# A state-space scan in front of a squared-ReLU layer: the first loads reordered, unit 0's masks on one engine, and the order of work up to unit 5 written anew

## The chip, the cores and the metric

One Trainium2 chip, one of its cores. The metric is the time of one execution on the device in microseconds (us). The engines of the core run side by side, each through its own list of instructions in order: TensorE (PE in the profile; PEld is its weight load), VectorE (DVE), ScalarE (ACT), GpSimd (POOL) and SyncE (SP). SP, ACT and POOL issue DMA transfers; SPq, ACTq and POOLq are the rows of these issues. An instruction waits at the head of its engine's list until what it reads is there and what it overwrites has been read; everything behind it on that engine waits too.

## The reference

Inputs: x (4 batches, 8 heads, 768 steps, 32 wide), a (4, 8, 768), B and C (4, 8, 768, 16), w_in (256 x 2048), w_out (2048 x 256), all fp32. Per batch and head, over the steps in chunks of 32:

```python
log_a = np.log(np.clip(a, 1e-06, 1.0))
cum = np.cumsum(la, axis=-1)                       # la: log_a of this chunk
L = np.exp(cum[:, :, :, None] - cum[:, :, None, :]) * causal
M = np.einsum('bhin,bhjn->bhij', Cc, Bc) * L
y_intra = np.einsum('bhij,bhjd->bhid', M, xc)
y_inter = np.einsum('bhin,bhnd->bhid', Cc, state) * np.exp(cum)[:, :, :, None]
y[:, :, sl] = y_intra + y_inter
state = decay_full * state + np.sum(Bx, axis=2)    # Bx: outer(B, x), decayed to the chunk's end
```

Then y is laid out as 3072 tokens of 256 numbers, and the result is `relu(y @ w_in)**2 @ w_out`, 3072 x 256 in fp32.

## The kernel before, in words

**Units.** The 768 steps are cut into three parts of 256 (j), and a unit is one part of one batch: 12 units, numbered 0 to 11 as (b, j) with the batch running fastest, so units 0 to 3 are the first 256 steps of the four batches. A part of 256 steps is two chunks of 128 in the kernel's sense (i = 0, 1), and a state goes from chunk to chunk. Even and odd steps lie side by side in one partition (the index r, 0 or 1).

**Decay.** The products of a are taken as a running product rather than as sums of logarithms. `a_nat[0]` (64 partitions x 128) holds a of units 0 to 3, `a_nat[1]` (128 x 128, "late a") that of all others. `clamp` (L473) limits it, `scan` (L479) runs the product along 128 steps into `cp`; both are on VectorE. `prep_p` (L455) transposes `cp` on TensorE; for units 0 to 3 the result P0 is in PSUM bank 4 (token `sp`), for the rest it is `P_sb[:, :, 32:96]` (token `p`). `inv` (L560) takes reciprocals into `Pinv`. Totals of a chunk go to `Ptot` (`su`, `to`; later `pn`, `pt`) and, spread over heads, to `Pquad` (`fq`, L536, on GpSimd; later `pq`).

**A unit's steps**, with their tokens and lines:
- `ldB`, `ldC`, `ldx` (L127): load B, C (128 KB each) and x (256 KB); `:l` and `:h` load the lower or upper four heads alone. For units 4 on `ld` loads all three on SP. `gB`, `gC`, `gx` (L136) write one element of the tile from GpSimd first, so that the load waits until GpSimd has come that far in its list.
- `pc` (L160): C times P into the tile jt; `pb` (L170 on ScalarE, L172 on GpSimd): B cast into jt, with `pbl` and `pbh` for one half of the heads; `jz`: jt set to zero before its first use. `px` (L179): xs = x times Pinv.
- `tr` (L197): transposes of jt on TensorE, `tc` (L210 ScalarE, L212 VectorE): copies of them from PSUM to bct. For unit 0, `trC`/`tcC` and `trB`/`tcB` do C and B apart. From unit 4 on `tr` is a DMA transpose.
- `mt` (L222): scores C·B into PSUM banks 0 to 3, one bank for each q = 0 to 3. `mk` (L231): VectorE multiplies one bank by the causal mask. Instead of that, `sc` (L236) copies a bank by ScalarE, and `ms` (L240) masks the copy on the engine named.
- `u` (L247): a chunk's contribution to the state; `sf` (L359) and later `za`, `zb`, `sa`, `sb`: states, with Sd the decayed state; `us` (L310): a copy of the contribution.
- `in` (L247): the intra-chunk product, which needs all four masked banks and xs; `ina` and `inb` are its halves over two banks each. `ca` (L247): the product with the state.
- `t` (L210, L212, L296): the unit's y copied from PSUM to T, the right-hand side of the next product. `rg` does u, ca, in, mt and t of neighbouring units together, from unit 4 on.

**The layer.** Letters a to l are the units. `a0` is the first product of unit 0 with columns group 0 of w_in: four matmuls (L406) and a ReLU on ScalarE (L411); `qa0` squares it on VectorE (L417); `A0` is the second product with w_out, four matmuls (L433). Groups 0 to 7 complete a unit; `A7` also copies and stores the result. The weights come by four transfers each from GpSimd's queue: `wi0` to `wi3` (L141; wi0 serves groups 0 and 1, and so on), `wo0` to `wo3` (L145).

**The order.** Nothing sorts the work: the string ORDER is read from left to right by `one`, and each token appends its instructions to the lists of its engines. `:a`, `:v`, `:p`, `:s` name the engine (ScalarE, VectorE, GpSimd, SyncE), `@` gives the PSUM banks. So the order on an engine, DMA issues included, is that of its tokens in the string. `id3:512@5` (L486) issues three matmuls of 512 columns into bank 5 whose result nobody reads; they keep TensorE busy at the start. `ef`, `eb`, `ti`, `pi`, `ku`, `hd`, `mb` build constants (identity, mask and the like), `wm` makes ScalarE load its table and copy one small tile, `pk` sets two constants for the totals.

What loads late a, and what scans it:

```python
def late_a():
    SQ.dma_start(out=a_nat[1], in_=_dap(a, 256, [[128, 4], [S, 32], [1, 128]]))
def scan(m):
    if m not in clamped:
        clamp(m)
    V.tensor_tensor_scan(out=cp[m], data0=a_cl[m], ...)
```

Of the kernel before, what the change touches and what calls it, by code (L numbers as in the profile page):

```python
# [30 lines left out]
def kernel(  # L31
# [16 lines left out]
    ORDER = """
        id3:512@5 fa1:a la fa0:s ku ef ldx0:h:a eb id2:512@5 ti id1:512@5 gB3 pi ldB0:l:a hd ldC0:l:a ldB0:h:s ldC0:h:s
        ldx0:l:a wm jz0:v mb jz1:v ldB1:s id3:512@5 sk pbh0:a id1:512@5 pk pbl0:p wi0 sp trB0@7 tcB0:2:a ldC1:s  # L50
        id7:192@0 pc0:v iv1:0:8 cl1 px0:p trC0@36 ps wi1 su tcC0:1:a tcC0:0:v mt0 u0@675 iv:8:16 pb1:a to fq us0 sc0
        pc1:p sn1 mk0 mk0 mk0 id5:512@4 tr1@41 ms0:p tc1:1:v sf0 ldx1:s tc1:0:a wi2 px1:p wo0 mt1 in0 ldB2:s ca0 mk1 mk1
        mk1 t0:aa p2@4 a1@5 a0@4 u1@612 mk1 sf1 ldC2:s ina1 inb1 ca1 a2@3 t1:vv pn us1 a3@7 pt@0 qa2 b0@5 jz2:p qa1 b2@4
        qa3 qa0 b3@6 pb2:a b1@2 qb0 pc2:v wo1 gx2 ldx2:s ldB3:s ldC3:s qb1 qb2 a4@7 a5@0 wi3 b4@3 qa5 tr2@41 B0 A0
        tc2:1:a iv:32:64 iv:16:32 qb3 qa4 tc2:0:a b5@5 zb1 B1 A1 mt2 B2 ldx3:s B3 A3 sc2 A2 qb4 qb5 mk2 mk2 b7@0 wo2
        ms2:v sb1 mk2 qb7 a6@5 a7@4 pb3:a wo3 px2 ld4 b6@2 A4 A5 pc3:v qa6 u2@45 ina2 inb2 tr3@31 B5 B4 zb0 sb0 qa7 ld6
        sf2 tc3:1:v qb6 pc4:p tc3:0:a ca2 pb4:p tr4 ld5 px3:v pq t2:aa us2 A6 mt3 u3@45 mk3 us3 A7 mk3 c0@4 za3 mk3 c6@0
        c5@7 B6 sa3 mk3 pc5:p afC2 pb5 tr5 ld7 c1@2 qc0 px5:p px4:v qc1 zb2 qc6 qc5 c2@4 B7 c7@1 pb6:p c3@3 C0 c4@0 C5
        rg4@56 qc2 qc4 qc3 mk4 C2 C4 C1 qc7 mk4 mk4 d7@0 qd7 d0@6 d1@5 d2@2 qd0 za4 C3 d4@0 d6@4 qd2 mk4 iv:64:96 zb4
        sa4 d5@1 C6 qd1 qd6 C7 d3@6 qd4 qd5 zb3 rg5@45 D0 mk5 e0@6 za5 mk5 pc6 D6 e2@0 D5 sa5 px6 qe0 qd3 mk5 zb5 pc7  # L60
        px7 D4 D2 e3@6 sb3 sb5 sb2 mk5 e1@0 D1 tr6 qe2 D3 pb7 ld8 qe1 sb4 rg6@56 D7 e4@4 qe3 za6 sa6 tr7 zb6 mk6 e5@5
        qe4 sb6 e6@6 qe5 e7@4 qe6 mk6 E0 E1 E2 E3 ld9 px8 mk6 f0@5 qe7 E4 f1@6 qf0 pc8 E5 pb8 E6 mk6 f2@4 qf1 f3@5 qf2
        E7 rg7@46 mk7 F0 f4@5 qf3 za7 tr8 F1 F2 f5@6 qf4 f6@4 qf5 f7@5 qf6 g0@6 qf7 zb7 sa7 sb7 mk7 F3 mk7 F4 pc9 pb9
        px9 ld10 g1@4 qg0 F5 mk7 g2@5 qg1 F6 g3@6 qg2 F7 rg8@45 za8 zb8 sa8 sb8 g4@6 qg3 G0 mk8 tr9 g5@4 qg4 G1 mk8 g6@5
        qg5 G2 g7@6 qg6 G3 mk8 h0@4 qg7 G4 pc10 pb10 px10 ld11 h1@5 qh0 G5 mk8 h2@6 qh1 G6 h3@4 qh2 G7 rg9@56 za9 zb9
        sa9 sb9 h4@4 qh3 H0 mk9 tr10 h5@5 qh4 H1 mk9 h6@6 qh5 H2 h7@4 qh6 H3 mk9 i0@5 qh7 H4 pc11 pb11 px11 i1@6 qi0 H5
        mk9 i2@4 qi1 H6 i3@5 qi2 H7 rg10@46 za10 zb10 sa10 sb10 i4@5 qi3 I0 mk10 tr11 i5@6 qi4 I1 mk10 i6@4 qi5 I2 i7@5
        qi6 I3 mk10 j0@6 qi7 I4 j1@4 qj0 I5 mk10 j2@5 qj1 I6 j3@6 qj2 I7 rg11@45 za11 zb11 sa11 sb11 j4@6 qj3 J0 mk11
        j5@4 qj4 J1 mk11 j6@5 qj5 J2 j7@6 qj6 J3 mk11 k0@4 qj7 J4 k1@5 qk0 J5 mk11 k2@6 qk1 J6 k3@4 qk2 J7 rg12@56 k4@4
        qk3 K0 k5@5 qk4 K1 k6@6 qk5 K2 k7@4 qk6 K3 l0@5 qk7 K4 l1@6 ql0 K5 l2@4 ql1 K6 l3@5 ql2 K7 l4@6 ql3 L0 l5@4 ql4  # L70
        L1 l6@5 ql5 L2 l7@6 ql6 L3 ql7"""
# [49 lines left out]
    def ph_load(k, what, eng=None, hs=(0, 8)):  # L121
        b, j = UNITS[k]
        src, w = {"B": (B, N), "C": (C, N), "x": (x, D)}[what]
        t = loaded.setdefault(k, {})
# [2 lines left out]
        (eng or nc.sync).dma_start(  # L127
            out=t[what][:, hs[0]:hs[1]],
            in_=_dap(src, ((b * NH + hs[0]) * S + j * 256) * w, [[2 * w, 128], [S * w, hs[1] - hs[0]], [1, 2 * w]]))
# [329 lines left out]
    with tc.manual_schedule():  # L459
# [103 lines left out]
        def first_a(u, eng):  # L563
            load_a(u, eng)

        def late_a():
            SQ.dma_start(out=a_nat[1], in_=_dap(a, 256, [[128, 4], [S, 32], [1, 128]]))
# [196 lines left out]
```

## Time and profile before

| | us |
|---|---|
| median of 3 runs | 115.98 |
| lowest, highest of them | 114.93, 139.79 |
| the profiled execution | 114.99 |
| its span | 113.1 |
| TensorE busy, 1626 matmuls | 107.9 (95%) |
| VectorE, ScalarE, GpSimd busy | 84.5 (75%), 76.1 (67%), 47.2 (42%) |

The span is the time from the profile's zero to the last instruction; the profiled execution's own time is 1.9 us longer. Busy time is no measure of what bounds a stage: TensorE's contains the matmuls that only keep it busy, and their ends are modelled. The chain of waits goes back from the last instruction to what released it and so on; its rows are start, length, and what. In a timeline a row is start, length, engine, line, operation, written tile and read tile; a bracket at its end gives the idle time of the engine before it and what ended that. A row of the DMA view gives a transfer's size and the time from its issue to its landing.

### The profile page before, as it was taken

How to read it: one execution, taken by the hardware profiler on the slowest of the kernel's cores; microseconds unless marked ns; L12 is line 12 of the kernel's file. 1: busy time of each engine (PE TensorE's matmuls, PEld its weight loads, DVE VectorE, ACT ScalarE, POOL GpSimd, SP SyncE). 2: the span in 40 equal slices, each digit the busy share in tenths (PEclk: the TensorE clock that was granted, in tenths of full speed). 3: DMA queues.
4: the chain of work that ended last, by engine and by line, in shares of the span. 5: the costliest groups of instructions: out<-in, count | busy, mean ns of one | idle time of the engine just before them, and what ended most of it. 6: DMA issues, size and time to landing. Idle time of an engine off the chain costs nothing.

```text
span 113.1 us, 4000 instructions
## 1 busy us (share of the span) xinstructions
PE 107.9 (95%) x1626; PEld 93.6 (83%) x1626; DVE 84.5 (75%) x192; ACT 76.1 (67%) x160; POOL 47.2 (42%) x98
## 2 busy tenths in 40 slices
...
GB/s 21 203 178 197 181 161 166 187 158 183 186 204 230 85 215 208 177 37 176 171 95 126 132 110 164 79 151 20 0 171 0 6 96 0 41 58 0 93 0 93
DMA packets 47814, 13.46 MB, mean 119 GB/s; under 512 B 44276, under 2 KB 45876, under 8 KB 47796
## 3 DMA queue, kind: packets, MB, share of 16 engines
...
q10 hardware_dynamic: 2304, 0.48, 2.0%
q8 instruction: 12, 0.20, 0.7%
q14 instruction: 6, 0.05, 0.1%
HBM read 10.58 MB, written 3.15 MB: 121 GB/s over the span
## 4 chain that ended last, share of the span: by engine, by line
PE 87%; DVE 3%; DMA 3%; POOL 3%; ACTq 1%; issue 0%; ACT 0%; POOLq 0%
PE pp L433 38%; PE pp L406 37%; PE pp L247 7%; PE pp L222 4%; DMA B_nat<-in_B_dram 3%; DVE mts L231 2%; PE pp L197 1%; POOL xs L179 1%; POOL w_in_b L141 1%; POOL jt L160 1%; DVE jt L160 1%; PE pp L455 0%; ACTq L127 0%; ACTq L117 0%; PE pp L552 0%
## 5 line engine op out<-in xcount | busy, mean ns | idle before, releaser
L411 ACT ACTIVATE hb<-pp 128x512 bf16<-128x512 f32 x96 | 54.8, 600 | 22.8 <-PE pp L406 20.8
L417 DVE TENSOR_TENSOR h<-hb 128x512 bf16<-128x512 bf16 x96 | 45.0, 490 | 13.2 <-ACT hb L411 12.8
L433 PE MATMUL pp<-w_out_b,h 128*128 128x256 bf16 (+1 forms) x400 | 53.9, 268 | 0.0
L406 PE MATMUL pp<-T,w_in_b 128*128 128x256 bf16 x384 | 53.2, 273 | 0.1
L406 PEld LDWEIGHTS <-w_in_b 128*128 128x128 bf16 x384 | 41.7, 114 | 1.8 <-issue 0.8
L433 PEld LDWEIGHTS <-h 128*128 128x128 bf16 x400 | 37.5, 98 | 4.4 <-issue 0.6
L231 DVE TENSOR_TENSOR mts<-pp,mask 128x512 bf16<-128x512 f32 x46 | 30.4, 681 | 1.5 <-PE pp L222 1.5
L347 POOL TENSOR_TENSOR Sd<-z,Pquad 128x256 bf16<-128x256 f32 x16 | 11.2, 706 | 33.8 <-DVE z L331 23.7
L179 POOL TENSOR_TENSOR xs<-x_nat,Pinv 128x256 bf16<-128x256 f32 (+1 forms) x17 | 12.8, 767 | 2.5 <-DMA x_nat<-in_x_dram 2.2
L160 POOL TENSOR_TENSOR jt<-C_nat,P_sb 128x128 bf16<-128x128 f32 x18 | 7.8, 451 | 4.7 <-DMA C_nat<-in_C_dram 4.7
L486 PE MATMUL pp<-const-bfloat16-1.0 128*128 128x512 bf16 (+1 forms) x22 | 6.3, 445 | 0.8 <-PEq L748 0.8
L440 ACT COPY osb<-pp 128x512 f32<-128x512 f32 x11 | 6.4, 585 | 0.5 <-PE pp L433 0.4
L331 DVE SCALAR_TENSOR_TENSOR z<-z,Ptot,us 128x64 f32<-128x64 f32 x8 | 2.6, 328 | 5.4 <-ACT us L315 5.4
L172 POOL CAST jt<-B_nat 128x128 bf16<-128x128 f32 x17 | 5.4, 343 | 2.3 <-DMA B_nat<-in_B_dram 2.3
L247 PE MATMUL pp<-mts,xs 64*32 64x128 bf16 x384 | 6.1, 219 | 0.1
L222 PE MATMUL pp<-bct 32*64 32x256 bf16 x192 | 5.1, 279 | 0.6 <-DVE bct L212 0.5
L296 ACT CAST T<-pp 128x512 bf16<-128x512 f32 x7 | 4.1, 585 | 1.7 <-PE pp L247 1.4
L486 PEld LDWEIGHTS <-const-bfloat16-1.0 128*128 128x128 bf16 x22 | 2.3, 117 | 3.4 <-issue 3.0
L247 PEld LDWEIGHTS <-xs 64*32 64x32 bf16 x384 | 4.3, 90 | 0.6 <-issue 0.4
L247 PE MATMUL pp<-bct,Sd 128*128 128x128 bf16 x40 | 4.2, 220 | 0.0
L210 ACT COPY bct<-pp 128x384 bf16<-128x384 bf16 (+1 forms) x6 | 2.6, 450 | 1.6 <-PE pp L197 1.6
L497 ACT ACT_TABLE_LOAD x1 | 1.3, 1283 | 3.6 <-issue 3.6
...
## 6 DMA issues: line engine op xcount, KB each, us to landing
x_nat<-in_x_dram SPq DMA_DIRECT2D x11, 256.0 KB, 3.5
out_dram<-osb SPq DMA_DIRECT2D x11, 256.0 KB, 3.1
B_nat<-in_B_dram SPq DMA_DIRECT2D x11, 128.0 KB, 2.8
C_nat<-in_C_dram SPq DMA_DIRECT2D x11, 128.0 KB, 2.9
w_in_b<-in_moe_w_in_dram POOLq DMA_DIRECT2D x4, 256.0 KB, 5.4
w_out_b<-in_moe_w_out_dram POOLq DMA_DIRECT2D x4, 256.0 KB, 4.7
x_nat<-in_x_dram ACTq DMA_DIRECT2D x2, 128.0 KB, 3.6
bct<-jt SPq DMA_TRANSPOSE x8, 3.4
```

The costliest lines, as they stand in the source:

```text
L160: eng.tensor_tensor(out=_fap(jt[k % 3], 128 + 144 * g, [[384, 2], [32, 4], [1, 16]]), in0=_fap(loaded[k]["C"], 128 * g, [[16, 2], [32, 4], ...
L179: eng.tensor_tensor(out=_fap(xs, 256 * r, [[256, 2 // n], [32, 8], [1, 32]]), in0=_fap(loaded[k]["x"], 32 * r, [[32, 2 // n], [64, 8], [1, ...
L222: nc.tensor.matmul(pp[64 * u:64 * u + 64, q, r * 256:r * 256 + 256], bct[32 * q:32 * q + 32, r, 0, u * 64:u * 64 + 64], _fap(bct[32 * q:32 ...
L231: nc.vector.tensor_tensor(out=live[k]["mts"][:, q].rearrange("p r g i -> p (r g i)"), in0=pp[:, q, :], in1=mask, op=ALU.mult)
L247: nc.tensor.matmul(dst, w, v, start=bool(need), stop=False, skip_group_check=True, **({} if pos is None else {"tile_position": pos}))
L347: nc.gpsimd.tensor_tensor(out=_fap(S_d, 0, [[128, 2], [32, 4], [1, 32]]), in0=_fap(z, 0, [[32, 2], [0, 4], [1, 32]]), in1=_fap(Pquad, 4 * ...
L406: nc.tensor.matmul(pp[:, h, i * 256:(i + 1) * 256], _fap(w, g * w.shape[2] + (o // 2) * 512 + 2 * (o % 2) + i, [[4, 128]]), T[blk][:, g].r ...
L411: nc.scalar.activation(out=hb.rearrange("p i t -> p (i t)"), in_=pp[:, h, :], func=AF.Relu)
L417: nc.vector.tensor_tensor(out=h2, in0=hb, in1=hb, op=ALU.mult)
L433: nc.tensor.matmul(dst, h2[:, i, r * 128:(r + 1) * 128], w_out_b[gi][:, 2 * o + i, c0:c1], start=first, stop=(fp == 7 and i == 1), skip_gr ...
L440: nc.scalar.copy(out=osb, in_=pp[:, 6 if blk == 1 else 7, :])
L486: nc.tensor.matmul(pp[:, h, 0:int(cols)], ones_b[:, 0:128], ones_b[:, 0:int(cols)] if dep is None else dep, start=True, stop=True, skip_gr ...
```

## The change

ORDER is written anew up to the token `C5` of unit 2 (behind it, from `rg4@56` on, it is the same), and late a can be loaded in four parts.

- **First loads.** Before: ACT issues the second piece of first a, x0's upper half, B0 low, C0 low, x0 low, and then loads its table (`wm`); SP issues late a whole, first a's other piece, B0 high, C0 high, B1, C1, x1, B2, C2. After: ACT issues first a's piece, C0 low, B0 low, then `wm`, then x0 low; SP issues first a's other piece, C0 high, late a's part 3, B0 high, part 1, B1, part 2, C1, x0 high, part 0, x1, B2, C2, B3.
- **Late a** is four transfers of 32 rows (`lq0` to `lq3`) in place of one (`la`).
- **Unit 0's masks.** Before: three on VectorE; the fourth bank is copied by ScalarE (`sc0`) and masked by GpSimd (`ms0:p`). After: all four on VectorE. The clamp and scan of late a (`cl1`, `sn1`) stood ahead of them on VectorE and now stand behind them; the memset of jt1 (`jz1`) now stands just ahead of them.
- **Unit 1** is transposed through banks 4 and 6 in place of 4 and 1, and its two copies `tc1:0` and `tc1:1` change places between ScalarE and VectorE.
- **Up to unit 5**: B of unit 2 is cast by GpSimd and not by ScalarE (`pb2`), B3 is loaded earlier, a4, a5 and b4 come behind unit 2's transposes, B2 before its scores, `pc3` before the last mask of unit 2 (`ms2`), and other products of units 0 and 1 change places. The number of products is the same; the matmuls that only keep TensorE busy are in other places.

```diff
-        id3:512@5 fa1:a la fa0:s ku ef ldx0:h:a eb id2:512@5 ti id1:512@5 gB3 pi ldB0:l:a hd ldC0:l:a ldB0:h:s ldC0:h:s
-        ldx0:l:a wm jz0:v mb jz1:v ldB1:s id3:512@5 sk pbh0:a id1:512@5 pk pbl0:p wi0 sp trB0@7 tcB0:2:a ldC1:s
-        id7:192@0 pc0:v iv1:0:8 cl1 px0:p trC0@36 ps wi1 su tcC0:1:a tcC0:0:v mt0 u0@675 iv:8:16 pb1:a to fq us0 sc0
-        pc1:p sn1 mk0 mk0 mk0 id5:512@4 tr1@41 ms0:p tc1:1:v sf0 ldx1:s tc1:0:a wi2 px1:p wo0 mt1 in0 ldB2:s ca0 mk1 mk1
-        mk1 t0:aa p2@4 a1@5 a0@4 u1@612 mk1 sf1 ldC2:s ina1 inb1 ca1 a2@3 t1:vv pn us1 a3@7 pt@0 qa2 b0@5 jz2:p qa1 b2@4
-        qa3 qa0 b3@6 pb2:a b1@2 qb0 pc2:v wo1 gx2 ldx2:s ldB3:s ldC3:s qb1 qb2 a4@7 a5@0 wi3 b4@3 qa5 tr2@41 B0 A0
-        tc2:1:a iv:32:64 iv:16:32 qb3 qa4 tc2:0:a b5@5 zb1 B1 A1 mt2 B2 ldx3:s B3 A3 sc2 A2 qb4 qb5 mk2 mk2 b7@0 wo2
-        ms2:v sb1 mk2 qb7 a6@5 a7@4 pb3:a wo3 px2 ld4 b6@2 A4 A5 pc3:v qa6 u2@45 ina2 inb2 tr3@31 B5 B4 zb0 sb0 qa7 ld6
-        sf2 tc3:1:v qb6 pc4:p tc3:0:a ca2 pb4:p tr4 ld5 px3:v pq t2:aa us2 A6 mt3 u3@45 mk3 us3 A7 mk3 c0@4 za3 mk3 c6@0
-        c5@7 B6 sa3 mk3 pc5:p afC2 pb5 tr5 ld7 c1@2 qc0 px5:p px4:v qc1 zb2 qc6 qc5 c2@4 B7 c7@1 pb6:p c3@3 C0 c4@0 C5
+        ef id3:512@5 fa0:s ku fa1:a ldC0:l:a eb ldC0:h:s ldB0:l:a wm gB3 ti lq3:s ldB0:h:s hd jz0:v ldx0:l:a lq1:s
+        ldB1:s id3:128@2 lq2:s pi id3:512@0 ldC1:s ldx0:h:a sk pbl0:p sp pbh0:a id2:512@5 pc0:v trC0@36 iv1:0:8 mb
+        trB0@7 tcC0:1:a lq0:s tcC0:0:v wi0 id7:192@0 tcB0:2:v ps mt0 jz1:v id1:512@4 px0:p wi1 pk iv:8:16 su mk0 to mk0
+        u0@675 ldx1:s mk0 fq pb1:a us0 mk0 pc1:p wi2 id1:128@6 id5:512@4 px1:p tr1@46 sn1 tc1:0:v tc1:1:a mt1 sf0 in0
+        ca0 wo0 mk1 t0:aa p2@4 mk1 ldB2:s mk1 a1@5 a0@4 ldC2:s mk1 ldB3:s u1@612 sf1 pn ina1 inb1 ca1 t1:vv a2@3 us1
+        pt@0 a3@7 jz2:p pb2:p b2@4 qa2 qa1 b0@5 b3@3 pc2:v gx2 ldx2:s qa3 qa0 b1@2 qb0 ldC3:s tr2@41 qb1 a4@7 a5@0 b4@3
+        tc2:0:a iv:16:32 qb2 B0 qa5 A0 tc2:1:a zb1 qb3 iv:32:64 wo1 qa4 A1 ldx3:s wi3 b5@5 B1 wo2 qb5 B2 mt2 sc2 mk2 A3
+        mk2 sb1 mk2 pc3:v A2 b7@4 a6@5 B3 qb7 wo3 a7@4 qb4 px2 A5 ms2:v pb3:a qa6 b6@2 qa7 u2@45 ina2 inb2 ld4 pb4:p
+        tr3@10 sf2 pc4:p B5 zb0 ld6 qb6 tc3:1:v ca2 A4 us2 tc3:0:a px3:v sb0 B4 tr4 A6 mt3 t2:aa ld5 mk3 u3@45 us3 A7
+        c0@4 c6@0 za3 sa3 B6 pb5 mk3 mk3 pq mk3 c5@7 pc5:p tr5 afC2 ld7 c1@2 qc0 px5:p px4:v qc1 zb2 qc6 qc5 c2@4 B7
+        c7@1 pb6:p c3@3 C0 c4@0 C5
...
+        def late_a_part(u, eng):
+            eng.dma_start(out=a_nat[1][32 * u:32 * u + 32, :], in_=_dap(a, 256 + u * 128, [[S, 32], [1, 128]]))
...
-                "la": late_a,
+                "la": late_a, "lq": lambda: late_a_part(k, eng),
```

More of the change, by code (lines that the diff above doesn't have):

```diff
@@ L59 @@
[L59 to L68, printed above, removed]
@@ L69 @@
-        j5@4 qj4 J1 mk11 j6@5 qj5 J2 j7@6 qj6 J3 mk11 k0@4 qj7 J4 k1@5 qk0 J5 mk11 k2@6 qk1 J6 k3@4 qk2 J7 rg12@56 k4@4
-        qk3 K0 k5@5 qk4 K1 k6@6 qk5 K2 k7@4 qk6 K3 l0@5 qk7 K4 l1@6 ql0 K5 l2@4 ql1 K6 l3@5 ql2 K7 l4@6 ql3 L0 l5@4 ql4
-        L1 l6@5 ql5 L2 l7@6 ql6 L3 ql7"""
+        ef id3:512@5 fa0:s ku fa1:a ldC0:l:a eb ldC0:h:s ldB0:l:a wm gB3 ti lq3:s ldB0:h:s hd jz0:v ldx0:l:a lq1:s
+        ldB1:s id3:128@2 lq2:s pi id3:512@0 ldC1:s ldx0:h:a sk pbl0:p sp pbh0:a id2:512@5 pc0:v trC0@36 iv1:0:8 mb
@@ new lines @@
+        mk2 sb1 mk2 pc3:v A2 b7@4 a6@5 B3 qb7 wo3 a7@4 qb4 px2 A5 ms2:v pb3:a qa6 b6@2 qa7 u2@45 ina2 inb2 ld4 pb4:p
+        tr3@10 sf2 pc4:p B5 zb0 ld6 qb6 tc3:1:v ca2 A4 us2 tc3:0:a px3:v sb0 B4 tr4 A6 mt3 t2:aa ld5 mk3 u3@45 us3 A7
+        c0@4 c6@0 za3 sa3 B6 pb5 mk3 mk3 pq mk3 c5@7 pc5:p tr5 afC2 ld7 c1@2 qc0 px5:p px4:v qc1 zb2 qc6 qc5 c2@4 B7
+        c7@1 pb6:p c3@3 C0 c4@0 C5 rg4@56 qc2 qc4 qc3 mk4 C2 C4 C1 qc7 mk4 mk4 d7@0 qd7 d0@6 d1@5 d2@2 qd0 za4 C3 d4@0
+        d6@4 qd2 mk4 iv:64:96 zb4 sa4 d5@1 C6 qd1 qd6 C7 d3@6 qd4 qd5 zb3 rg5@45 D0 mk5 e0@6 za5 mk5 pc6 D6 e2@0 D5 sa5
@@ new lines @@
+        px6 qe0 qd3 mk5 zb5 pc7 px7 D4 D2 e3@6 sb3 sb5 sb2 mk5 e1@0 D1 tr6 qe2 D3 pb7 ld8 qe1 sb4 rg6@56 D7 e4@4 qe3 za6
+        sa6 tr7 zb6 mk6 e5@5 qe4 sb6 e6@6 qe5 e7@4 qe6 mk6 E0 E1 E2 E3 ld9 px8 mk6 f0@5 qe7 E4 f1@6 qf0 pc8 E5 pb8 E6
+        mk6 f2@4 qf1 f3@5 qf2 E7 rg7@46 mk7 F0 f4@5 qf3 za7 tr8 F1 F2 f5@6 qf4 f6@4 qf5 f7@5 qf6 g0@6 qf7 zb7 sa7 sb7
+        mk7 F3 mk7 F4 pc9 pb9 px9 ld10 g1@4 qg0 F5 mk7 g2@5 qg1 F6 g3@6 qg2 F7 rg8@45 za8 zb8 sa8 sb8 g4@6 qg3 G0 mk8
+        tr9 g5@4 qg4 G1 mk8 g6@5 qg5 G2 g7@6 qg6 G3 mk8 h0@4 qg7 G4 pc10 pb10 px10 ld11 h1@5 qh0 G5 mk8 h2@6 qh1 G6 h3@4
```

6 lines of the change are left out of this document (added).

## The prediction

> **What bounds the kernel now.** I read the page first, then the chain of waits of the first 50 us, then the timelines of the engines and DMA issues up to 16 us. Times are us from the start of the span.
>
> ```profile
> span 113.1 us, 4000 instructions
> ...
> PE 87%; DVE 3%; DMA 3%; POOL 3%; ACTq 1%; issue 0%; ACT 0%; POOLq 0%
> ```
>
> The profiled execution took 114.99 us: 113.1 of span and 1.9 around it. The median of the three runs shown is 115.98, the lowest 114.93, so my sum stands against the low end; a measurement here tells about 2% (2.3 us) from no change. TensorE (PE) holds 87% of the chain. What is left is at the start:
>
> ```profile
> 5.54 0.45 PE pp L455 x8
> ...
> 6.86 1.04 POOL xs L179
> 7.90 0.72 POOL w_in_b L141
> ...
> 8.64 0.25 POOL Pquad L536
> 8.89 0.72 POOL jt L160 x2
> ...
> 9.66 0.41 PE pp L197 x4
> ...
> 10.09 0.37 DVE bct L212
> ...
> 10.51 0.55 PE pp L222 x16
> 11.05 2.49 DVE mts L231 x4
> ...
> 13.58 0.62 PE pp L247 x17
> 14.20 0.87 PE pp L406 x8
> ...
> 21.04 0.35 PE pp L222 x16
> ```
>
> Columns are start, length, what. From 13.58 the chain is TensorE work without a gap worth naming. 13.58 is `inb1`, the second half of unit 1's intra product; it waits for the last of the four masks of unit 1. The set of useful TensorE work ahead of `inb1` is the same in both orders (units 0 and 1, the first-sums, `p2`, a0, a1), and the work behind it is the same too. So the change is worth what it moves the start of `inb1`, plus any stall that it makes later. The path to `inb1` is GpSimd (POOL), not VectorE: it forms xs of unit 0 at 6.86, issues a weight load, forms Pquad, then unit 1's C (8.89 to 9.61); transposes, scores and masks follow. From xs0's start to `inb1` this is 13.58 - 6.86 = 6.72.
>
> **The loads.** The next two views give the issues (start, length) and the time from an issue to its landing.
>
> ```profile
> 0.81 0.39 ACTq L117 DMA_DIRECT2D a_nat<-in_a_dram  x1
> 0.81 0.75 SPq L567 DMA_DIRECT2D a_nat<-in_a_dram  x1
> 1.61 0.42 SPq L117 DMA_DIRECT2D a_nat<-in_a_dram  x1
> 2.54 0.52 SPq L127 DMA_DIRECT2D C_nat<-in_C_dram  x1
> 3.01 0.52 ACTq L127 DMA_DIRECT2D x_nat<-in_x_dram  x1
> 3.56 1.28 ACT L497 ACT_TABLE_LOAD   x1 [3.56 <-issue]
> 4.82 0.38 SPq L127 DMA_DIRECT2D C_nat<-in_C_dram  x1
> 4.85 0.19 ACT L497 COPY warm<-warm 128x2 bf16<-128x2 bf16 x1
> 15.43 4.35 SPq L127 DMA_DIRECT2D C_nat<-in_C_dram  x1
> ```
>
> ```profile
> a_nat<-in_a_dram ACTq DMA_DIRECT2D x1, 16.0 KB, 1.7
> a_nat<-in_a_dram SPq DMA_DIRECT2D x1, 16.0 KB, 3.0
> B_nat<-in_B_dram SPq DMA_DIRECT2D x1, 64.0 KB, 3.4
> x_nat<-in_x_dram ACTq DMA_DIRECT2D x1, 128.0 KB, 3.5
> C_nat<-in_C_dram SPq DMA_DIRECT2D x1, 128.0 KB, 2.9
> x_nat<-in_x_dram SPq DMA_DIRECT2D x1, 256.0 KB, 5.5
> C_nat<-in_C_dram SPq DMA_DIRECT2D x1, 128.0 KB, 9.7
> ```
>
> In the old order the lower half of x0, ACT's fifth load, lands at 3.01 + 3.5 = 6.5, and xs0 starts at 6.86.
>
> Four pieces of late a in place of one transfer cost SP 4 x 0.42 = 1.68 of issue for 0.75. Three stand ahead of x0's upper half, which is now SP's ninth issue: behind first a and three pieces (4 x 0.42), C0 (0.52), B0 (0.42 assumed), B1 and C1 (0.38 each), with eight steps of 0.03, it is issued at 0.81 + 3.62 = 4.43. Its price is between C1's 2.9 (as many bytes) and x0's 3.5: it lands between 7.3 and 7.9. The lower half, on ACT, stands behind the table load. With 0.39, two 64 KB issues at 0.52, the table's 1.28, the copy's 0.19 and five steps of about 0.03 it is issued at 0.81 + 3.05 = 3.86 and at 3.5 lands at 7.4. I take 7.5 for both halves and 7.55 for the start of xs0, **0.69 later than now**. What unit 0 gains elsewhere doesn't hide this, since xs0, wi1, Pquad and unit 1's C keep their order on GpSimd.
>
> The Trainium skill, DMA: Bandwidth & Descriptors, section "Rules for kernel authors", would have many small transfers coalesced into one, which speaks against the four pieces. The 0.42 rows agree: by that rule one transfer at 0.75 ahead of x0 in place of three pieces would bring it 0.5 earlier.
>
> **VectorE's path.** Its rows:
>
> ```profile
> 2.05 0.38 DVE L684 MEMSET jt<- 128x384 uint32 x1
> 4.72 0.22 DVE L473 TENSOR_SCALAR a_cl<-a_nat 64x128 f32<-64x128 f32 x1 [1.04 <-DMA a_nat<-in_a_dram]
> 4.97 0.42 DVE L479 TENSOR_TENSOR_SCAN cp<-a_cl,const-float32-0.0 64x128 f32<-64x128 f32 x1
> 6.01 0.59 DVE L160 TENSOR_TENSOR jt<-C_nat,pp 128x128 bf16<-128x128 f32 x2 [0.62 <-PE pp L455]
> 6.68 0.16 DVE L473 TENSOR_SCALAR a_cl<-a_nat 128x128 f32<-128x128 f32 x1
> 7.28 0.24 DVE L560 RECIPROCAL Pinv<-P_sb 128x16 f32<-128x16 f32 x1
> 7.43 0.75 DVE L479 TENSOR_TENSOR_SCAN cp<-a_cl,const-float32-0.0 128x128 f32<-128x128 f32 x1
> 10.37 0.41 DVE L359 TENSOR_TENSOR Sd<-pp,Pquad 128x256 bf16<-128x256 f32 x1
> ```
>
> ```profile
> 0.85 4.32 PE L486 MATMUL pp<-const-bfloat16-1.0 128*128 128x512 bf16 x10 [0.85 <-PEq L748]
> ```
>
> First a now leads both queues. By ACT's 1.7 it lands at 2.5 (by SP's 3.0 at 3.8); clamp and scan with their step take 0.67, so its cumulative product is there at 3.2. TensorE's fillers ahead of `sp` take 0.85 + 6 x 0.43 + 3 x 0.11 = 3.8 by the ten that took 4.32, so `sp` starts at about 3.8 and not at 5.54, and `pc0` at 4.3 where it was 6.01. C0 has 16 KB ahead of it in each queue; at 3.4 from 1.25 it lands at 4.65 at the latest. `pc0` ends near 5.0. B0's upper half is SP's fourth issue, 2.25 + 3.4 = 5.65 at worst, 5.0 if it lands in C1's 2.9 or a little under. A cast at half of `pc0`'s 0.59, the transposes and a copy at unit 1's 0.41 and 0.37 make 1.07 more: `mt0` starts between 6.1 and 6.7. I take 6.3; it frees VectorE's first mask 0.54 later (10.51 to 11.05 in unit 1).
>
> That advance is spent on VectorE. Behind the copy at about 6.25 come the memset of jt1 (0.38) and a reciprocal (0.24): 6.87. Then four masks, 2.49 by unit 1's row, where now three stand and the fourth goes over ACT and GpSimd: 9.36. Then the clamp (0.16) and the scan (0.75), which stood ahead of the masks: 10.27. Then the copy and Sd, 0.69 together by their rows (10.09 to 10.78): 10.96. There VectorE could start unit 1's masks, against 11.05 now. **So with GpSimd in time the whole front gains 0.1;** with `mt0` at 6.1 or 6.7 it is 0.3 or -0.3.
>
> GpSimd loses one piece, the mask product of the copied score, but that stands behind unit 1's C now and off the path. Its end sets only wi2 and xs1, which have room: wi2 and xs1 would follow C1 at once.
>
> **The sum.** Unit 1's C ends on GpSimd at 9.61 + 0.69 = 10.30, later than VectorE is done with its scan, so GpSimd goes on setting the path. The two copies of unit 1's transposes change engines; the later one is now ACT's:
>
> ```profile
> 9.92 0.48 ACT L210 COPY bct<-pp 128x384 bf16<-128x384 bf16 x1 [0.85 <-PE pp L197]
> ```
>
> 0.48 against VectorE's 0.36 adds 0.12. `inb1` starts at 7.55 + 6.72 + 0.12 = 14.39: +0.81.
>
> Behind it the order is anew up to unit 5, with the same products. One more group of four (B2, 0.44 from 0.87 for eight) stands ahead of `mt2`: 21.04 + 0.81 + 0.44 = 22.3. Of what is moved, one wait is new: `pc3` stands on VectorE behind three masks of unit 2, ahead of two squares and the fourth mask. The masks end at 22.3 + 0.54 + 3 x 0.62 = 24.7; C3 landed at 15.43 + 9.7 = 25.1. By that row VectorE waits 0.4 and passes about half of it on to unit 2's intra; with B3 no longer ahead of C3 on SP it waits for nothing. I take nothing; beyond 25.1 each us of C3 is a us for the squares and the second half of the intra. GpSimd now forms unit 2's B ahead of wo1 and wi3; B2 was cast by ACT before. By 25 us the same bytes have to come in either order, and B3 ahead of x2 only changes places. I take 0 here, between -0.2 and +0.9 (the rival on C3). 114.99 + 0.81 = **115.8**.
>
> **The rivals.**
>
> x0 lands early, VectorE bounds. If both halves land by 6.6 (2.2 to 2.7 behind their issue), C1 is done by 9.4 and unit 1's masks start at VectorE's 10.96. Time 114.99 - 0.1 = 114.9, 114.7 with `mt0` early. For it: on SP 16 KB behind the late a took 3.0 where on ACT 16 KB at the head took 1.7. So 1.3 of SP's price may be the transfer ahead, which is split and put back now. Against it: ACT's own 128 KB took 3.5 with no late a ahead, and here it is issued behind the table load.
> The Trainium skill, same page, section "Why a DMA increments its semaphore by 16 and not by 1", says that a DMA runs on as many of the 16 engines as divide its slowest dimension: the old late a, with four groups outermost, on 4 and the pieces of 32 rows on 16. By that rule this rival gains; the two rows agree with it, but no view here shows the engine of a packet.
>
> x0 lands late, and this ends slower. x0 now shares the queues with B1, C1 and the first weights. x1's price, 5.5, was that of a load beside them. By it the upper half lands at 4.43 + 5.5 = 9.9, xs0 starts at 9.95, 3.1 behind now, and `inb1` at 16.8: time 118.2. It decides (over 2%) from a landing of 9.0 on. Against: the weights' queue starts behind GpSimd's cast of B0, and C1, right ahead in the queue, took 2.9.
>
> C3 comes late to VectorE. If its landing slips to 26, by the 0.9 of the chain's shift, `pc3` blocks two squares and the last mask of unit 2 for 0.9 and TensorE with them: 116.7. For it: C3's issue alone took 4.35. Against: one load fewer (B3) stands ahead of it.
>
> The change does not do what it says. Unit 0's masks may come no earlier if B0 or C0 keep their 3.4 and first a SP's 3.0. Then `mt0` is at 6.7, and VectorE's path reaches 11.4, still below GpSimd's 11.86: the same 115.8.
>
> **How the numbers follow.** The forecast, with the rival of the same time, has 0.57: x0 lands between 7.1 and 8.1, time 115.3 to 116.5. x0 early 0.20, x0 late 0.10, C3 late 0.08; 0.05 is for what no row here prices. The range 114.6 to 117.2 holds all but x0 late and that rest: its low end is VectorE's floor, its high end C3 late with x0 half a us later. Faster by over 2% needs `inb1` at 11.3, ahead of VectorE's own floor of 13.3: 0.03. Slower by over 2%: x0 late and a part of the rest, 0.11. Same 0.86.
>
> **What would show it.** Right: `sp` near 3.8, `mt0` near 6.3, VectorE's four masks from about 6.9 to 9.4 and the scan to 10.3, xs0 at about 7.5, waiting for a DMA of x; C1 done on GpSimd near 10.3; unit 1's masks from about 11.9; `inb1` at 14.4, TensorE without gaps behind it. Wrong: xs0 before 7.0 with VectorE holding unit 1's masks (x0 early), xs0 after 8.5 (x0 late), a gap of TensorE between 20 and 30 that VectorE's `pc3` or a weight ends, or a place of `inb1` that moves one way while the time moves the other.

## The result, and the profile after

The changed kernel takes 116.12 us in the median of 20 runs; the kernel before, on the same chip, 115.08 (20 runs). The ratio is 1.0070, with a 95% interval of 1.0042 to 1.0098: the change makes the kernel slower by 0.7%, well under the 2% of the verdict but outside what these runs leave uncertain. The ratio leaves out executions over 1.5% above the fastest of the same kernel (here 157.6 and 117.05, before 139.79) and compares the means of the others (115.97 and 115.16), so it is not the quotient of the two medians. The profiled execution took 115.79 us.

**A correction first.** The words ahead of the prediction and the prediction itself make SP the issuer of x0's upper half after the change. The token is `ldx0:h:a`: ScalarE issues both halves. The term of the sum that hung on this is the one that failed.

The top of the page, and the chain of waits up to unit 3 (start, length, what):

```profile
span 114.1 us, 4006 instructions
...
PE 87%; DMA 5%; DVE 2%; issue 2%; SPq 1%; ACT 1%; ACTq 0%; DVEq 0%
```

```profile
1.26 2.58 DMA C_nat<-in_C_dram
3.86 0.37 SPq L127
...
5.36 2.77 DMA a_nat<-in_a_dram
8.13 1.20 DVE mts L231 x2
9.33 1.04 issue
10.37 0.24 DVE a_cl L473
...
10.97 0.34 DVE bct L212
...
14.37 0.62 PE pp L247 x17
...
29.50 0.54 PE pp L433 x4
```

GpSimd, which had 3% of the chain before, is gone from it. In its place stand loads (C0, then a part of late a) and VectorE. From 14.37 (`inb1`) on it is TensorE again. The row at 29.50 is A7, the end of unit 0; before, it was this one:

```profile
28.84 0.54 PE pp L433 x4
```

So A7 comes 0.66 later, and the last group of matmuls is 0.66 later as well (108.60 against 107.94). The rest of the span's 1.0, some 0.35, is added at the very end. The last store is issued here (kernel before, then changed):

```profile
110.53 0.37 ACTq L723 DMA_DIRECT2D out_dram<-osl  x1
```

```profile
111.18 0.37 ACTq L726 DMA_DIRECT2D out_dram<-osl  x1
```

Both land 1.7 behind their issue, but from the end of the issue to the end of the span it is 2.2 before and 2.55 after. The traces of all versions fall into two groups by this time: 2.2 to 2.3 with late a in one transfer, 2.5 to 2.6 with late a in four, whatever the order. What it consists of no view shows, and since what lies between the span and the execution's own time varies from 1.7 to 2.4, neither is it shown how much of it reaches that time.

The next rows are from the timelines of the engines, sorted by start:

```profile
2.37 1.28 ACT L497 ACT_TABLE_LOAD   x1 [2.37 <-issue]
2.65 0.96 ACTq L127 DMA_DIRECT2D x_nat<-in_x_dram  x2
3.81 0.64 PE L455 MATMUL pp<-eye_f,cp 64*64 64x32 f32 x8
4.96 0.91 POOL L141 DMA_DIRECT2D w_in_b<-in_moe_w_in_dram  x1 [0.26 <-issue]
5.36 0.77 SPq L570 DMA_DIRECT2D a_nat<-in_a_dram  x1
6.12 1.04 POOL L179 TENSOR_TENSOR xs<-x_nat,Pinv 128x512 bf16<-128x512 f32 x1 [0.25 <-DVE bct L212]
6.37 0.42 PE L222 MATMUL pp<-bct 32*64 32x256 bf16 x16
6.84 2.48 DVE L231 TENSOR_TENSOR mts<-pp,mask 128x512 bf16<-128x512 f32 x4
8.10 0.76 POOL L160 TENSOR_TENSOR jt<-C_nat,P_sb 128x128 bf16<-128x128 f32 x2
10.37 0.23 DVE L473 TENSOR_SCALAR a_cl<-a_nat 128x128 f32<-128x128 f32 x1 [1.04 <-issue]
10.63 0.42 DVE L479 TENSOR_TENSOR_SCAN cp<-a_cl,const-float32-0.0 128x128 f32<-128x128 f32 x1
11.36 0.42 PE L222 MATMUL pp<-bct 32*64 32x256 bf16 x16 [1.46 <-DVE bct L212]
11.83 2.48 DVE L231 TENSOR_TENSOR mts<-pp,mask 128x512 bf16<-128x512 f32 x4 [0.20 <-PE pp L222]
24.70 0.50 DVE L160 TENSOR_TENSOR jt<-C_nat,P_sb 128x128 bf16<-128x128 f32 x2 [0.37 <-DMA C_nat<-in_C_dram]
```

ScalarE's table load (2.37 to 3.65) runs beside its two issues of x0 (from 2.65), so x0 was there by 6.1 and GpSimd starts xs0 0.74 earlier than before, not 0.69 later. Unit 1's C is ready on GpSimd at 8.86. What unit 1 waits for is VectorE: its four masks end at 9.33, then it is idle for 1.04 until the clamp of late a, and the scan and the copy of unit 1's transposes stand behind that. TensorE is idle for 1.46.

What the clamp waits for is read in two ways. The chain names no releaser ("issue") and lets a load issued at 5.36 end at 8.13. The DMA view, which has one transfer issued there, part 0 of late a (`lq0`), gives its size and a longer time from issue to landing:

```profile
a_nat<-in_a_dram SPq DMA_DIRECT2D x1, 16.0 KB, 4.9
```

By this it lands at 10.26, though it has 16 KB, and the clamp starts at 10.37. The DMA view is taken here, since part 0 is the one load that the clamp needs and that is issued so late. Between 7 and 8 us the two kinds of queues shared the engines so, in the changed kernel and in the kernel before (packets, MB, share of the 16 engines; q0 carries GpSimd's weights, q1 the loads that SP issues; ScalarE's go over q10, which moves nothing in this stretch):

```profile
q0 software_dynamic: 115, 0.12, 105.7%
q1 hardware_dynamic: 70, 0.01, 7.6%
```

```profile
q1 hardware_dynamic: 724, 0.17, 76.3%
q0 software_dynamic: 3, 0.00, 2.3%
```

The first weights, issued at 4.96 where it was 5.67, now hold the engines in the very stretch in which the rest of SP's queue should land. In this execution part 0 is among what lands late.

### The profile page after: what moved, and what is told of

It reads as the page before. It is cut to its first block, busy times and chain, and to the rows that moved or that the text cites. A ratio compares the mean times of both kernels' runs of the same rounds, so it can differ in the third digit from the quotient of the medians.

```text
span 114.1 us, 4006 instructions
## 1 busy us (share of the span) xinstructions
PE 107.6 (94%) x1628; PEld 94.0 (82%) x1629; DVE 84.3 (74%) x194; ACT 74.8 (66%) x156; POOL 46.7 (41%) x99
## 4 chain that ended last, share of the span: by engine, by line
PE 87%; DMA 5%; DVE 2%; issue 2%; SPq 1%; ACT 1%; ACTq 0%; DVEq 0%
PE pp L406 38%; PE pp L433 37%; PE pp L247 7%; PE pp L222 3%; DMA a_nat<-in_a_dram 2%; DMA C_nat<-in_C_dram 2%; DVE mts L231 1%; SPq L127 1%; PE pp L197 1%; ACT T L210 1%; SPq L570 1%; ACTq L117 0%; DVE bct L212 0%; ACT osl L725 0%; DVE a_cl L473 0%
## 5 line engine op out<-in xcount | busy, mean ns | idle before, releaser
L417 DVE TENSOR_TENSOR h<-hb 128x512 bf16<-128x512 bf16 x96 | 44.5, 483 | 13.1 <-ACT hb L411 12.7
L231 DVE TENSOR_TENSOR mts<-pp,mask 128x512 bf16<-128x512 f32 x47 | 30.9, 682 | 2.2 <-PE pp L222 2.1
L486 PE MATMUL pp<-const-bfloat16-1.0 128*128 128x512 bf16 (+2 forms) x24 | 6.5, 407 | 1.5 <-PEq L751 0.8
L222 PEld LDWEIGHTS <-bct 32*64 32x64 bf16 x192 | 1.9, 102 | 2.8 <-DVE bct L212 1.8
L210 ACT CAST T<-pp 128x256 bf16<-128x256 f32 x8 | 2.6, 381 | 1.8 <-PE pp L247 1.8
```

Of the source, the lines that this page charges most:

```text
L222: nc.tensor.matmul(pp[64 * u:64 * u + 64, q, r * 256:r * 256 + 256], bct[32 * q:32 * q + 32, r, 0, u * 64:u * 64 + 64], _fap(bct[32 * q:32 ...
L231: nc.vector.tensor_tensor(out=live[k]["mts"][:, q].rearrange("p r g i -> p (r g i)"), in0=pp[:, q, :], in1=mask, op=ALU.mult)
L417: nc.vector.tensor_tensor(out=h2, in0=hb, in1=hb, op=ALU.mult)
L486: nc.tensor.matmul(pp[:, h, 0:int(cols)], ones_b[:, 0:128], ones_b[:, 0:int(cols)] if dep is None else dep, start=True, stop=True, skip_gr ...
```

## The experiments

Ratios are to the kernel before on the same chip.

**The change again.** The same kernel once more; nothing is edited.

> The changed kernel itself once more, beside the three others on one chip. Theory: 0.5 to 1.2 above the kernel before; the landing of late a's last part, or of C1 right ahead of it, differs from one execution to the next by a microsecond or more, and inb1 with it, while the issue times on SP stay within 0.1.

Ratio 1.0136 [1.0096, 1.0176], so the loss is there again, and more of it. Its profiled execution (115.27 us) is one in which part 0 came in time:

```profile
9.26 0.21 DVE L473 TENSOR_SCALAR a_cl<-a_nat 128x128 f32<-128x128 f32 x1
9.51 0.42 DVE L479 TENSOR_TENSOR_SCAN cp<-a_cl,const-float32-0.0 128x128 f32<-128x128 f32 x1
10.95 2.48 DVE L231 TENSOR_TENSOR mts<-pp,mask 128x512 bf16<-128x512 f32 x4 [0.41 <-PE pp L222]
12.12 1.04 POOL L179 TENSOR_TENSOR xs<-x_nat,Pinv 128x512 bf16<-128x512 f32 x1 [2.33 <-DMA x_nat<-in_x_dram]
```

Part 0 was issued only 0.12 earlier (5.24) and landed 2.4 behind that, so the clamp waits for nothing; the first weights came at 5.42, 0.46 later than in the trace above. Between 7 and 8 SP's queue had even less of the engines here (3.0%, the weights 64.8%), so that share alone does not make part 0 late. x1 is late in both traces (5.9 and 5.3 behind its issue, xs1 waiting 2.33 and 2.02 for it). The times spread (115.27 to 117.47): which loads are late differs in part from execution to execution, and what the executions without a trace waited for is not known.

**x0's upper half on SP**, as the prediction had read it:

```diff
-... ldC1:s ldx0:h:a sk ...
+... ldC1:s ldx0:h:s sk ...
```

> The changed kernel with x0's upper half on SP, behind C1, which is how the prediction read the new order. If xs0's start carries inb1 with it at a distance of 6.7 to 6.9, as the prediction's sum has it, xs0 starts at 8.3 or later (issue near 5.3, at least 2.9 to land) and inb1 at 15.1 or later, 0.7 or more above the changed kernel. If the place of the load does not matter, xs0 starts near 6.2 as in the changed kernel and the time is the same.

Ratio 1.0238 [1.0194, 1.0283]. The chain and GpSimd's timeline:

```profile
4.85 2.90 DMA x_nat<-in_x_dram
...
16.27 0.62 PE pp L247 x17
```

```profile
7.93 1.04 POOL L179 TENSOR_TENSOR xs<-x_nat,Pinv 128x512 bf16<-128x512 f32 x1 [1.71 <-DMA x_nat<-in_x_dram]
```

The landing price was right (2.9), and xs0 does carry `inb1` when x0 is late. It does so by another way than the prediction's, which went over GpSimd's C: that was ready at 10.79, and the chain goes over unit 0's contribution (TensorE, 9.02), its copy on ScalarE (9.38) and the matmuls that only keep TensorE busy (9.70 to 12.06). The step to `inb1` is 8.34 where the prediction took 6.72 + 0.12. TensorE's clock was low in that stretch (granted 0.63 from 9 to 12, 0.71 from 12 to 14), which is a part of the difference; how large a part is not shown. The forecast for what I had misread was too low as well.

**Part 0 earlier in SP's queue**, ahead of C1:

```diff
-... lq2:s pi id3:512@0 ldC1:s ... lq0:s ...
+... lq2:s lq0:s pi id3:512@0 ldC1:s ...
```

> The changed kernel with one token moved: late a's part 0 is issued on SP ahead of C1 instead of behind it. Theory (the scan waits for the last part of late a): the part lands by 8.5, VectorE's clamp of late a starts at the end of unit 0's fourth mask, 9.3 to 9.4 instead of 10.37, unit 1's masks near 11.0, inb1 near 13.5 instead of 14.37; time 0.6 to 0.9 below the changed kernel, about that of the kernel before. Rival (four masks in a row on VectorE, or GpSimd, hold the path anyway): clamp earlier, but inb1 stays at 14.2 or later and the time within 0.2 of the changed kernel.

Ratio 1.0109 [1.0051, 1.0167], about that of the faster three of its six executions (115.48 to 117.07); the trace is of the slowest, 118.36. The wait for part 0 is gone there and C1 takes its place in the chain:

```profile
5.25 5.54 DMA C_nat<-in_C_dram
...
10.92 0.77 POOL jt L160 x2
```

C1 lands at 10.79, as late as part 0 did (10.3). After the gap that this leaves TensorE runs at half clock for 2 us (last section). The first weights were issued at 4.98. So moving one load ahead made the next one late, which agrees with the stretch from 7 to 9 being what is short, and not the order inside SP's queue; it is one trace.

**The first weights later**, behind xs0 on GpSimd:

```diff
-... tcC0:0:v wi0 id7:192@0 ... px0:p wi1 ...
+... tcC0:0:v id7:192@0 ... px0:p wi0 wi1 ...
```

> The changed kernel with the first weight load issued on GpSimd behind xs of unit 0 instead of ahead of it, some 2 later. Theory A (the weights crowd SP's transfers): part 0 of late a, issued at 5.4 as before, lands by 8.5 instead of 10.3, the clamp starts at 9.4, and the time falls by up to 0.6, less what a1 waits for the weights. Theory B (its place behind C1 on SP's queue is what holds it): it still lands after 9.5 and the time does not fall.

Part 0 then lands at 8.32, 3.0 behind its issue. By itself this says little, since part 0 came in 2.4 with the weights in place too (the change again). x1 and B2, issued behind it, say more: both land 3.4 behind their issue, where in the traces with late a in four and the weights ahead it is 5.3 to 6.4. The weights do crowd SP's loads. But the ratio is 1.0193 [1.0156, 1.0230]. The clamp and the scan now run beside GpSimd's weight issue and xs1 (VectorE's and GpSimd's timelines):

```profile
9.76 0.87 DVE L473 TENSOR_SCALAR a_cl<-a_nat 128x128 f32<-128x128 f32 x1
10.65 1.27 DVE L479 TENSOR_TENSOR_SCAN cp<-a_cl,const-float32-0.0 128x128 f32<-128x128 f32 x1
```

```profile
9.80 0.76 POOL L141 DMA_DIRECT2D w_in_b<-in_moe_w_in_dram  x1
10.58 1.06 POOL L179 TENSOR_TENSOR xs<-x_nat,Pinv 128x512 bf16<-128x512 f32 x1
```

**Late a whole**, where part 3 stands:

```diff
-... lq3:s ... lq1:s ... lq2:s ... lq0:s ...
+... la ...
```

> The changed kernel with late a again as one transfer, on SP where the first of the four parts stood. Theory (the scan's wait): late a lands before 8, clamp at the end of the fourth mask, 0.6 to 0.9 below the changed kernel unless B0's upper half, now behind it, comes late. Rival (the four parts are what gets C0, B0 early): B0's upper half lands 1 later than in the changed kernel, mt0 starts at 7.2 instead of 6.4, and the time is no lower than the changed kernel's.

Ratio 1.0285 [1.0239, 1.0331]. The transfer behind it, B0's upper half, pays:

```profile
2.53 4.22 DMA B_nat<-in_B_dram
...
8.14 0.41 PE pp L222 x16
```

In the changed kernel that load takes 2.6, and `mt0` starts at 6.37. In this order splitting late a gains more than the 0.35 at the end that goes with it. (The Trainium skill, DMA: Bandwidth & Descriptors, section "Why a DMA increments its semaphore by 16 and not by 1", has a transfer run on as many of the 16 engines as divide its slowest dimension; worked out from that, an estimate, 4 for the whole and 16 for a part. The longer landing of B0 agrees in direction, though no view here shows the engine of a packet.)

**Parts 2 and 0 on ScalarE**, behind x0:

```diff
-... lq2:s ... ldx0:h:a ... lq0:s ...
+... ldx0:h:a lq2:a lq0:a ...
```

> The changed kernel with late a's parts 2 and 0 issued on ACT behind x0's two halves instead of on SP around C1. Theory (the last part of late a, queued behind C1 on SP, is caught by the first weight transfer's burst between 7 and 9, and VectorE's scan waits for it): both parts land by 7.2, C1 too, the clamp starts at the end of the fourth mask near 9.35 instead of 10.37, inb1 near 13.4 instead of 14.37; time 0.7 to 1.1 below the changed kernel, equal to the kernel before or up to 0.3 under it. Rival (something else, GpSimd's part or the order behind, makes the loss): time within 0.3 of the changed kernel.

Ratio 1.0101 [1.0065, 1.0136], the runs in two groups (near 115.4 and 116.4). In the profile the clamp stands at 9.36 without a wait and unit 1's masks start at 11.04, but C2 lands late (16.80) and unit 2's transposes wait for it:

```profile
7.17 9.63 DMA C_nat<-in_C_dram
```

**The scan behind unit 1**, with what reads it:

```diff
-... tr1@46 sn1 tc1:0:v ... t0:aa p2@4 mk1 ... sf1 pn ina1 ... a3@7 ...
+... tr1@46 tc1:0:v ... t0:aa mk1 ... sf1 sn1 ina1 ... t1:vv pn a2@3 us1 a3@7 p2@4 ...
```

> The changed kernel with the scan of late a taken off the path: it stands on VectorE behind unit 1's four masks, and p2 and the totals' constant move behind a3. Theory: unit 1's masks start near 10.9 instead of 11.83 whenever late a lands, inb1 near 13.4; time 0.7 to 1.2 below the changed kernel. Rival (the wait for late a is no cause): inb1 moves by the scan's own 0.65 at most, time 0.4 or less below.

Ratio 1.0151 [1.0126, 1.0176]. Unit 1's masks start at 10.94, as meant; A7 comes at 30.09 all the same. The clamp takes 0.68 beside GpSimd's memset, and TensorE waits for what the scan gives (0.23 for `pick_p`, 0.42 for `P_sb`) and 0.53 for T, ahead of a1 and a0, where `p2` stood.

**The fourth mask off VectorE** again:

```diff
-... us0 mk0 pc1:p ...
+... us0 sc0 pc1:p ms0:p ...
```

> The changed kernel with unit 0's fourth mask off VectorE again: ScalarE copies the bank and GpSimd masks the copy, behind unit 1's C. Theory (the wait for late a binds, not the masks): VectorE comes to the clamp 0.62 earlier and waits that much longer; time within 0.3 of the changed kernel. Rival (four masks in a row are the loss): inb1 0.6 earlier, time 0.5 to 0.7 below.

Ratio 1.0170 [1.0137, 1.0202]. VectorE comes to the clamp at 8.93, but the scan takes 1.28 beside GpSimd's mask product (9.04 to 10.19), so unit 1's masks start at 11.25. GpSimd's weight issues move back too, and wi3 lands at 23.37, where TensorE waits 0.66 for it.

**The two halves of the order.** The new front (up to `ca1`, B3 not early) with the order of before behind it, and the reverse:

```diff
-(changed kernel) ... mk1 ldB3:s u1@612 ... ca1, then its own order
+(front alone)    ... mk1 u1@612 ... ca1, then the order of before from there
-(before)         ... ldC2:s ina1 inb1 ca1, then its own order
+(rest alone)     ... ldC2:s ldB3:s ina1 inb1 ca1 pn, then the changed order from there
```

> The changed order up to the token ca1 of unit 1 (without the early load of B3), and the order of the kernel before from there on. Theory (the whole loss lies ahead of inb1): inb1 at 14.3 to 14.4, and 0.6 to 1.0 above the kernel before. Rival (the order behind unit 1 costs): 0.4 or less above the kernel before.

> The order of the kernel before up to ca1 of unit 1 (with the early load of B3 added), and the changed order from there on. Theory (the loss is made ahead of inb1 and by loads that the new front brings late): inb1 at 13.6, C2 lands near 13 and unit 2's transposes do not wait; within 0.3 of the kernel before. Rival (the new order behind unit 1 costs by itself, as unit 2's transposes stand ahead of a4, a5, b4): 0.4 or more above the kernel before.

The front alone: 1.0049 [1.0023, 1.0076]. In its profile part 0 is in time, `inb1` starts at 13.38, 0.2 earlier than before, and A7 at 28.79, 0.05 earlier; the span is 0.3 longer all the same (113.4), all of it behind the last store's issue (2.57 from its end). So in this trace the front loses nothing but what goes with the four parts. The profiled execution (115.33) is one of its faster ones (median 115.63).

The rest alone: 1.0124 [1.0099, 1.0149]. `inb1` stands where it stood, and then C3's product (`pc3`), which waits on VectorE ahead of unit 2's last mask (chain, then TensorE's timeline):

```profile
14.88 10.27 DMA C_nat<-in_C_dram
...
25.17 0.91 DVE jt L160 x2
...
26.75 0.35 DVE mts L240
...
30.38 0.54 PE pp L433 x4
```

```profile
27.14 0.40 PE L247 MATMUL pp<-mts,xs 64*32 64x128 bf16 x15 [0.89 <-DVE mts L240]
```

This is the prediction's rival on C3: VectorE waits 1.33, TensorE 0.89. In the changed kernel the same product waits only 0.37 (24.70, above), because the front is later and C3 landed at 24.7. The halves therefore don't add: 0.5% and 1.2% alone, 0.7% to 1.4% together.

**C3's product alone, from both sides.** First the rest alone with that one token put back, then the kernel before with that one token moved ahead:

```diff
-... mk2 pc3:v A2 ... ms2:v ...
+... mk2 A2 ... ms2:v pc3:v ...
```

```diff
-... ms2:v ... A5 pc3:v qa6 ...
+... pc3:v ms2:v ... A5 qa6 ...
```

> The order of before up to unit 1's intra product and the new order behind it, with one token put back: C3's product with P stands on VectorE behind the last mask of unit 2 and not ahead of it. Theory A (the rest costs because that product waits for C3 and holds the squares and the mask behind it): the TensorE gap of 0.89 that this mask ended goes, A7 starts near 29.3 to 29.6 in place of 30.38, ratio to the kernel before 1.002 to 1.006 where the rest alone gave 1.0124. Theory B (the loads themselves are late and something else of unit 2 or 3 waits as long): A7 stays above 30, ratio 1.010 to 1.014.

> The kernel before with one token moved: C3's product with P stands on VectorE ahead of unit 2's last scalar-copied mask, not behind three squares. Theory A: C3 lands at 25.1 as in before, where the mask stood at 23.7, so VectorE waits about 1.4 and half or more of it reaches TensorE: A7 starts 0.6 to 1.4 later than 28.84, ratio 1.005 to 1.012. Theory B: the place of this product costs nothing without the other edits: ratio 0.998 to 1.003.

Put back: 1.0066 [1.0040, 1.0093] where the rest alone gave 1.0124 [1.0099, 1.0149]; the intervals don't meet (the two ran on different chips, each against the kernel before on its own), though it is a little above the 1.002 to 1.006 expected. A7 goes from 30.38 to 29.57. Moved ahead in the kernel before: 1.0065 [1.0031, 1.0099], and the wait is there (VectorE's timeline):

```profile
24.79 0.49 DVE L160 TENSOR_TENSOR jt<-C_nat,P_sb 128x128 bf16<-128x128 f32 x2 [0.91 <-DMA C_nat<-in_C_dram]
```

Both agree that the place of this product costs about 0.6%, half of what the rest costs alone. A7 moved by 0.42 in the second, less than the 0.6 at least that was expected; its trace is of one of the faster executions (115.22, median 116.02), so most of that 0.65% lies in executions without a trace. The other half isn't this product's: with it put back, unit 2's contribution waits 0.20 for GpSimd's xs2, which waited for x2.

**B3's load put back** behind x2, in the rest alone:

```diff
-... ldC2:s ldB3:s ina1 ... gx2 ldx2:s ...
+... ldC2:s ina1 ... gx2 ldx2:s ldB3:s ...
```

> The order of before up to unit 1's intra product and the new order behind it, with B3's load put back behind x2's, as it stands in before. Theory A: B3 ahead of x2 makes SP wait for one landing more and so brings C3 later (25.14 measured): C3's landing changes by up to 1 us either way and the ratio follows the wait of C3's product, about 1.006 to 1.012. Theory B: B3's place changes nothing, because by 25 us the same bytes have to come: 1.011 to 1.014.

Inconclusive. The profiled execution, 115.44, fits an earlier C3 (24.48, A7 at 29.30), but it is the fastest of six that reach up to 119.78, and no trace of the others is there. The ratio is 1.0221 [1.0188, 1.0253]; whether the edit helps or hurts is open.

**Two further versions.** The first (`g2`) is the kernel before with unit 0's four masks on VectorE and late a's clamp and scan behind them; the second (`g3`) is the new front with parts 2 and 0 on ScalarE and the fourth mask off VectorE, and the order of before behind it.

```diff
-(before) ... cl1 px0:p ... us0 sc0 pc1:p sn1 mk0 mk0 mk0 ... ms0:p ...
+(g2)     ... px0:p ... us0 pc1:p mk0 mk0 mk0 mk0 sn1 ...
-(front alone) ... lq2:s ... ldx0:h:a ... lq0:s ... us0 mk0 pc1:p ...
+(g3)          ... ldx0:h:a lq2:a lq0:a ... us0 sc0 pc1:p ms0:p ...
```

> The kernel before with only the masks changed: all four of unit 0 on VectorE, clamp and scan of late a behind them; loads as they were. Four masks (2.49) in place of three (1.87) and the scan (0.75 to 0.9) behind them: unit 1's masks from 12.0 to 12.3 instead of 11.05, inb1 14.5 to 14.8; 0.8 to 1.2 above the kernel before. If GpSimd and not VectorE holds the path to inb1, as the prediction's first part had it: within 0.3.

> The new front with late a's parts 2 and 0 on ACT and unit 0's fourth mask off VectorE (ScalarE copy, GpSimd mask behind unit 1's C), and the order of the kernel before behind unit 1. If VectorE's chain to inb1 is what is left of the loss: inb1 near 12.9, time 0.3 to 0.6 below the kernel before. If the loads behind (C2, the weights) set the time from 14 on: inb1 early all the same, but the time within 0.3 of the kernel before or above it.

The first took 115.65 to 119.15, 118.0 in the median; in the profiled one (117.83) VectorE's scan ends at 11.98, TensorE waits 2.19 and runs at half clock from 15 to 17. Masks ahead of the scan don't pay without the earlier front. The second gave 1.0063 [1.0041, 1.0084]: its clamp, beside GpSimd's mask product, took 1.75.

**Four edits of the change together**: parts 2 and 0 on ScalarE, `pc3` behind `ms2`, unit 2's transposes behind a4, a5 and b4, B3 behind x2:

```diff
-... lq2:s ... ldx0:h:a ... lq0:s ... mk1 ldB3:s u1@612 ... ldx2:s ... tr2@41 qb1 a4@7 a5@0 b4@3 ... pc3:v A2 ... ms2:v ...
+... ldx0:h:a lq2:a lq0:a ... mk1 u1@612 ... ldx2:s ldB3:s ... qb1 a4@7 a5@0 b4@3 tr2@41 ... A2 ... ms2:v pc3:v ...
```

> The changed kernel with four edits: late a's parts 2 and 0 issued by ScalarE behind x0, C3's product behind the last mask of unit 2, unit 2's transposes behind a4, a5 and b4, B3's load behind x2's. Theory A (what the change loses is the wait for late a's part 0 and the waits for C2 and C3): unit 1's second intra product at 13.4 to 13.6 as in before, A7 near 28.8 to 29.0, ratio 0.998 to 1.004. Theory B (with the DMA engines full from 2.6 us on, each reordering makes another load late): the front is as good as that, but another load or weight ends a TensorE gap between 15 and 28, ratio 1.006 to 1.012.

Ratio 1.0115 [1.0080, 1.0149]; other loads come late instead, as the second theory had it. The front is as good as hoped (unit 1's masks at 10.89, where the changed kernel has 11.83), yet A7 comes at 30.17, since of the loads behind x1 lands at 11.82 and C3 at 26.46 (chain):

```profile
5.42 6.40 DMA x_nat<-in_x_dram
...
16.02 10.44 DMA C_nat<-in_C_dram
...
26.49 0.49 DVE jt L160 x2
```

No version that was run beats the kernel before. In those with late a in four parts some 0.3 of the span is lost behind the last store.

## Why the prediction was right and wrong

The forecast was a move of +0.81 to 115.8. Against the profiled execution it came to 115.79, and the ratio, 1.0070, is that of 115.8 to 114.99. The size was right, the reason was not: the agreement is luck.

- **First loads, `sp`, `mt0`, masks: right.** 3.81, 6.37 and 6.84 to 9.33, forecast 3.8, 6.3 and 6.87 to 9.36.
- **x0 and xs0: wrong.** This is the step that failed: "xs0 0.69 later than now". Both halves are ScalarE's, the table load doesn't hold its issues back, and xs0 came 0.74 earlier. With it fell "GpSimd goes on setting the path": C1 was done at 8.86, not 10.30. In its place, in the profiled execution, stands VectorE's wait of 1.04 for part 0 of late a, with unit 1's masks at 11.83. The rival "x0 lands early, VectorE bounds" named the right engine and gave it 0.20.
- **VectorE's path: right in order, wrong in two prices.** The scan was charged at 0.75, which it takes beside xs0; with GpSimd idle it takes 0.42. The clamp was assumed ready behind the masks; in the profiled execution it waited 1.04. The sum put unit 1's masks at 10.96 with GpSimd in time; the changed kernel without the late part has 10.95, with it 11.83. That second number matches the forecast of 11.86 by accident. No step asked when part 0 would land, though it was counted as an issue ahead of x0.
- **The copy on ScalarE, +0.12: not there.** Unit 1 waited for VectorE's copy at 10.97.
- **Behind `inb1`, taken as 0: near, but not for the reason given.** `inb1` to A7 took 15.13, before 15.26. The wait of 0.4 for C3 that was worked out and then dropped is in the trace with 0.37, without a gap on TensorE. With the front of before the same place costs about 0.6%, as the two experiments on that product show. So a change that ends the front's wait can uncover this one.
- **The end of the span: not in the sum.** The prediction added nothing behind the last store; 0.35 came there, in the trace.
- **"About what a measurement of this kernel can tell", 2%:** with 20 runs on each side the interval is ±0.28%, and the whole effect lies between.

Shown: x0 was issued by ScalarE and landed early, and VectorE, not GpSimd, ended the front; the product of C3 ahead of the mask costs when C3 is late; late a whole is worse in this order; the weights slow SP's loads behind them. Seen in one execution only: the wait for part 0. In the two traces with the first weights at 4.96 and 4.98 the load that SP issued at 5.25 to 5.36 is the late one (part 0, C1); where they came between 5.10 and 5.42, part 0 landed 2.4 to 3.2 behind its issue. That is an agreement of a few traces, and no run moved the weights by so little. Open: how the 0.7% is made up over the executions without a trace, what the 0.3 at the end is, and what makes up the second half of the rest's cost; x2 for xs2 is seen in one trace only.
